# A new order of 1489 tasks for one fused kernel: a long convolution and a state-space scan on one core

## The chip, the cores and the metric

The kernel runs on 1 core of one Trainium2 chip. Its time is device time in microseconds (us), the median of the timed runs. The engines are TensorE (PE, with its weight loads as PEld), VectorE (DVE), ScalarE (ACT), GpSimd (POOL) and SyncE (SP). SP and POOL issue nearly all transfers (DMAs); each engine works through its own instructions in the order in which the program gives them, and waits at one whose inputs or buffers aren't ready.

## The reference

Two independent heads over 2048 positions and 1024 channels, in bfloat16, written side by side into one output:

```
# head A: short convolution, gate, long convolution by FFT, gate
k_shift = sum over t of k_pad[:, t:t+S] * shift_k[:, 3-t]          # 4 taps
kv = k_shift * v
y  = irfft(rfft(kv padded to 2S) * rfft(ssm_k padded to 2S))[:S] + kv * ssm_D
a  = q * y
# head B: diagonal complex state-space layer
Lam_bar = exp(dt * Lam);  B_bar = ((Lam_bar - 1) / Lam) * B
h[t] = Lam_bar * h[t-1] + B_bar x[t]
b  = 2 * Re(C h) + x * Dskip
out = concat(a, b)
```

## The kernel before

The whole kernel is one table, `ORDER`, and a loop over it. Each word of the table is a task (`U.3.0.1`), with the buffers that it takes behind a colon: `p` numbers are the 8 banks of PSUM, `a` numbers the first of one or more 2 KB-per-partition units of an arena of 53 units in SBUF, `h` and `w` numbers three slots each for scanned states (`gslot`) and for constants of the FFT (`wslot`). The loop calls the function of the task, which emits its instructions on the engines; the order of the words is so the order on every engine, and the tile framework puts a wait where an instruction needs another's result or a buffer that is still read.

```
for word in ORDER.split():
    task, _, slots = word.partition(":")
    for code, n in re.findall(r"([a-z])(\d+)", slots):
        cur.setdefault(code, []).append(int(n))
    f, *args = task.split(".")
    E[f](*args)
```

Head B, by blocks of 128 positions (i from 0 to 15):

- `bl`, `bT`, `bc` (or `bcv`): load a block of B (SP), transpose it on PE (8 matmuls against the identity, L415), copy it from PSUM to the tile BT on ACT (L431) or DVE (L427, L429). `cl`, `cT`, `cc`, `cx` do the same for C and the tile CT. `x.i`: a transposing DMA of block i of x (L447).
- `wb`, `wbe`, `exp1`, `dve2`, `sin0`, `eo` and the like make the tables at the start. `eo` is 16 small ACT copies.
- `U.i.jp.jl`: 16 matmuls of 128x128 of x against BT (L464); two of them fill one bank, which `ue` copies to the arena (L473).
- `r1`, `r2`, `cy`, `sc`, `r3`, `r4`: rotation, the scan (L504, one pass per real and imaginary part) and rotation back, on DVE; `cy` carries the state over, on ACT.
- `y` (whole array, L520) or `yq` (four 64x64 quarters of the array at once, L538): the product with CT; `ye` copies it out; `yst`, `ysp`, `ysg`, `ysh` store it (POOL or SP).

Head A, as an FFT of three passes with a bounce through DRAM between each:

- `kp`, `vp` load k and v; `kvm`, `kva`, `kvb`, `kvc` form kv on DVE (L588 to L603); `am` is the first pass on PE (L608), `ae` copies (L614), `ast` stores to Ys_kv (L617). For the filter: `hl`, `hT`, `hc`, `hm` (L657), `he`, `hst` to Ys_h (L668).
- `lh`, `lk` load groups of 128 rows of Ys_h and Ys_kv (L677), `lw` the constants (L672). Each group needs rows of every store. `sh` and `sk` are the second pass (L688), `she` and `ske` copy (L697, L704), `sw` and `swp` swap rows by DMA (L708), `pr` multiplies (L714), `sa` transforms back (L726), `sae` copies, `vst` stores to Vs (L737).
- `vl` loads from Vs (L742), `a3` is the last pass (L754), `a3e` copies (L761), `qp` loads q, `qm` multiplies (L763), `ost` and `osp` store (L764, L765).

A copy out of PSUM stands on ACT; with a `v` behind its name (`saev`, `a3ev`) it stands on DVE. The functions themselves stay as they are; only the table changes.

Of the kernel before, what the change touches and what calls it, by code (L numbers as in the profile page):

```python
# [72 lines left out]
bT.2.1:p0 U.0.0.1 bT.3.0:p7 bc.5.0 bc.2.1 bc.5.1 kva.3 kring U.1.2.0:p5 bl.3.1:a23 cl.0.0:a14 bT.2.0:p2 bT.3.1:p0
bl.7.1:a46 ue.1.0:a34 U.0.2.1:p6 bc.3.1 bc.2.0 U.0.2.0 U.1.2.1 cl.3.0:a37 bl.7.0:a26 cl.1.0:a25 bT.7.1:p2 kvb.3:a22
bT.7.0:p0 ue.0.0:a23 bc.6.1 kp.-2 x.3:a21 U.0.1.0:p3 bc.3.0 gz stt cl.2.0:a12 cT.0.0:p4 bc.7.0 bc.7.1 U.0.1.1 U.0.3.0:p0
kvm.1:a15 ue.1.2 vp.1:a27 U.0.3.1 U.3.2.0:p1 ue.0.1 U.3.0.0:p3 z1 kvm.2:a42 z2 ld_Q U.1.1.1:p2 ue.0.2 ue.0.3 x.2:a52
U.1.1.0 cl.3.1:a13 kva.1 cT.1.0:p7 cl.2.1:a32 kva.2 kvb.1:a14 kvb.2:a39 ue.1.1 kvm.0:a15 rta kvc.3 U.3.0.1 cx.6.0 kva.0
# [5 lines left out]
am.1.0:p7p6 ae.1.1.0 ae.1.0.0 cT.3.0:p5 cx.4.0 r2.3:h2 cx.5.1 r4.0 cx.7.1 hT.0.1:p4 ue.2.0:a36 cx.4.1 cc.3.0 hT.0.4:p2
cy.1:h0 kvm.4:a14 hT.0.6:p7 hc.0.1:a22 am.2.0:p1p3 r1.1:a27 ae.2.1.0 U.2.3.1 ue.2.3 U.2.2.0:p5 kva.4 hc.0.4:a42 U.2.2.1
cx.6.1 ue.2.2 U.2.1.0:p3 cT.2.0:p2 hc.0.6:a32 cc.2.0 ae.2.0.0 U.2.1.1 ast.3 r2.1 ue.2.1 hT.0.2:p5 hT.0.3:p7 ast.1
hc.0.3:a18 hm.0.6.1:p4p2 hT.0.7:p0 he.0.6.1.1:a43 y.0.0.0:p3 y.0.0.1 hm.0.4.0:p2p6 hdv.0 hc.0.7:a12 he.0.6.1.0
hm.0.7.0:p4p1 hT.0.5:p0 he.0.4.0.1:a29 ast.2 hdv.1 sc.1.0 hT.0.0:p7 he.0.4.0.0 hst.0.4.0 hc.0.2:a20 y.0.0.2
he.0.7.0.0:a50 y.0.0.3 hc.0.0:a13 hm.0.6.0:p4p2 ye.0.0:a19 hm.0.4.1:p5p7 y.0.1.0:p6 y.0.1.1 y.0.1.2 y.0.1.3 vp.2:a34
kvb.4:a31 he.0.6.0.0 sc.1.1 he.0.4.1.1 vp.3:a26 r1.2:a14 he.0.4.1.0 he.0.7.0.1 hst.0.7.0 r3.1:a46 hm.0.0.1:p1p5
hst.0.4.1 hc.0.5:a42 he.0.6.0.1 r4.1 hm.0.0.0:p2p3 he.0.0.1.0:a48 cy.2:h1 r2.2 hm.0.5.1:p7p0 ye.0.1 he.0.5.1.1:a23  # L90
he.0.5.1.0 kp.3 he.0.0.1.1 kvm.6:a38 he.0.0.0.0 y.1.1.0:p4 kvc.4 y.1.1.1 hst.0.6.0 hst.0.6.1 kp.4 kva.6 hst.0.5.1
hm.0.5.0:p6p0 he.0.5.0.0 kvm.5:a14 y.1.1.2 he.0.0.0.1 kvb.6:a25 he.0.5.0.1 y.1.1.3 hm.0.7.1:p2p7 ye.1.1:a28 he.0.7.1.0
kva.5 am.4.0:p1p6 y.1.0.0:p4 he.0.7.1.1 x.4:a32 hm.0.3.0:p2p3 ae.4.0.0:a29 hm.0.3.1:p5p0 hst.0.0.1 hst.0.0.0
he.0.3.1.0:a36 kvc.6 y.1.0.1 he.0.3.1.1 hst.0.5.0 kvb.5:a12 sc.2.1 ae.4.1.0 he.0.3.0.1 kvm.7:a13 y.1.0.2 am.4.1:p1p7
hl.3.0:a40 he.0.3.0.0 hm.0.1.0:p5p0 y.1.0.3 he.0.1.0.0:a38 am.6.1:p5p6 ae.4.1.1 U.4.3.1:p7 he.0.1.0.1 ae.6.0.1:a17
hl.2.1:a44 U.4.3.0 kvc.5 ae.6.1.1 am.6.0:p6p5 U.4.0.0:p2 ae.4.0.1 ue.4.3:a23 U.4.1.1:p3 ae.6.0.0 hm.0.2.0:p0p6 ae.6.1.0
ye.1.0 kva.7 hm.0.1.1:p5p7 sc.2.0 hm.0.2.1:p1p4 hst.0.7.1 hl.3.1 he.0.2.0.0:a34 U.4.1.0 he.0.1.1.0 hl.2.0 he.0.2.1.1
# [5 lines left out]
y.2.0.2 kvm.8:a48 r4.3 y.2.0.3 he.1.7.1.0 ae.7.0.1 hc.1.2:a31 y.2.1.3 ye.2.0:a47 hm.1.4.1:p4p6 ae.7.1.1 kva.8
hm.1.7.0:p3p5 ye.2.1 yq.3.0:p1p0 hst.0.1.1 he.1.7.0.1 he.1.7.0.0 hm.1.4.0:p7p2 yst.2 he.1.4.1.0:a29 kvm.9:a39 lw.3:w1
kvb.8:a38 he.1.4.0.1 vp.4:a12 yq.3.1 yq.3.2 he.1.4.1.1 he.1.4.0.0 hm.1.3.0:p5p6 he.1.3.0.1:a15 hm.1.3.1:p3p4 he.1.3.1.0
hst.1.7.0 he.1.3.1.1 yq.3.3 hm.1.2.1:p7p6 x.6:a37 he.1.2.1.0:a19 kva.9 he.1.2.1.1 he.1.3.0.0 kvc.8 x.5:a36 lw.1:w2
kvb.9:a35 kvm.10:a47 U.6.1.0:p3 U.6.1.1 am.8.1:p6p7 ast.7 hst.1.7.1 r1.4:a40 kva.10 ae.8.1.1:a44 hst.1.4.1 ae.8.0.1
# [735 lines left out]
```

## Time and profile before

| | |
|---|---|
| timed runs | 343.4, 344.65, 345.7 us; median 344.65 |
| profiled execution, from first to last instruction | 343.2 us (its own time beside the span isn't given) |
| PE busy | 329.5 us, 5086 matmuls |
| DVE busy | 325.1 us, 263 instructions |
| ACT busy | 273.5 us, 519 instructions |
| POOL busy | 68.9 us, 111 instructions |
| DMA | 100.83 MB, 294 GB/s on average |

All times are of one profiled execution. Busy time is the sum over an engine's instructions; matmuls overlap, so that a start-to-start time tells more of PE than a duration. Lines of the profile give the start and the length of a group of like instructions, the engine, the source line, the operation, output<-input, and in brackets the idle time before it with what ended it.

### The profile page before, as it was taken

What the parts mean: (1) busy time and instruction counts of PE and PEld (TensorE: products, weight loads), DVE (VectorE), ACT (ScalarE), POOL (GpSimd) and SP (SyncE); (2) the same over time, 40 slices, a digit from 0 to 9 for tenths busy, and PEclk for the clock granted to TensorE, in tenths of its full rate; (3) what the DMA queues carried; (4) which work ended last, traced back from release to release, by engine and by line L of the source; (5) the groups of instructions that cost most, each with busy time, mean ns of one, the idle gap of its engine ahead of it and who ended that gap; (6) DMA issues with size and microseconds to landing.
All of it is one profiled execution on the core that took longest, in us unless ns stands there. A gap on an engine that the chain in (4) does not pass through costs nothing.

```text
span 343.2 us, 11813 instructions
## 1 busy us (share of the span) xinstructions
PE 329.5 (96%) x5086; PEld 230.2 (67%) x5105; DVE 325.1 (95%) x263; ACT 273.5 (80%) x519; POOL 68.9 (20%) x111
## 2 busy tenths in 40 slices
...
GB/s 177 352 351 208 315 281 283 155 318 365 368 269 198 264 263 295 233 261 343 313 353 282 270 339 212 369 272 311 280 314 276 216 326 378 327 335 284 375 346 274
DMA packets 62592, 100.83 MB, mean 294 GB/s; under 512 B 29422, under 2 KB 31614, under 8 KB 62540
## 3 DMA queue, kind: packets, MB, share of 16 engines
...
## 4 chain that ended last, share of the span: by engine, by line
PE 74%; ACT 15%; DMA 4%; issue 3%; DVE 3%; SPq 0%; POOL 0%; DVEq 0%; POOLq 0%
PE bank L464 25%; PE bank L538 19%; PE bank L520 10%; PE bank L754 4%; PE bank L688 4%; PE bank L726 4%; PE bank L608 2%; PE bank L657 2%; ACT BT L431 2%; ACT arena L614 2%; ACT arena L473 2%; ACT CT L439 2%; ACT arena L637 2%; DMA wslot<-a_c_W 1%; DMA arena<-arena 1%
## 5 line engine op out<-in xcount | busy, mean ns | idle before, releaser
L464 PEld LDWEIGHTS <-BT 128*128 128x128 bf16 x2048 | 117.8, 98 | 14.4 <-issue 9.9
L464 PE MATMUL bank<-arena,BT 128*128 128x128 bf16 x2048 | 125.4, 221 | 1.1 <-ACT BT L431 0.9
L538 PE MATMUL bank<-CT,gslot 64*64 64x512 bf16 x1408 | 86.6, 378 | 0.0
L504 DVE TENSOR_TENSOR_SCAN gslot<-rtab,gslot 128x1040 bf16<-128x1040 f32 x32 | 73.0, 2311 | 0.5
L538 PEld LDWEIGHTS <-gslot 64*64 64x64 bf16 x1408 | 36.9, 107 | 30.8 <-issue 1.9
L473 ACT CAST arena<-bank 128x512 bf16<-128x512 f32 x63 | 40.5, 660 | 13.8 <-PE bank L464 13.4
L614 ACT CAST arena<-bank 128x512 bf16<-128x512 f32 x64 | 37.2, 680 | 6.7 <-PE bank L608 4.0
L697 ACT CAST arena<-bank 128x512 bf16<-128x512 f32 x63 | 35.0, 617 | 5.9 <-issue 2.8
L520 PE MATMUL bank<-CT,gslot 128*128 128x512 bf16 x153 | 38.5, 380 | 0.3
L665 ACT CAST arena<-bank 128x512 bf16<-128x512 f32 x64 | 35.2, 631 | 3.1 <-PE bank L657 3.0
L714 DVE TENSOR_TENSOR arena<-arena 128x4096 bf16<-128x4096 bf16 x16 | 36.5, 2280 | 1.1 <-DMA arena<-arena 1.0
L487 DVE TENSOR_TENSOR arena<-gslot,Z 128x4096 bf16<-128x4096 bf16 x16 | 36.6, 2287 | 0.8 <-DVE gslot L504 0.2
L704 ACT CAST arena<-bank 128x512 bf16<-128x512 f32 x60 | 34.4, 621 | 3.2 <-PE bank L688 3.0
L734 ACT CAST arena<-bank 128x512 bf16<-128x512 f32 x60 | 32.4, 616 | 5.5 <-PE bank L726 5.3
L487 DVE TENSOR_TENSOR arena<-arena,Z 128x4096 bf16<-128x4096 bf16 x16 | 36.5, 2280 | 0.1
L556 ACT CAST arena<-bank 128x512 bf16<-128x512 f32 x31 | 18.1, 599 | 16.6 <-PE bank L538 8.7
L588 DVE TENSOR_TENSOR arena<-arena 128x4096 bf16<-128x4096 bf16 (+3 forms) x16 | 30.0, 1881 | 0.0
L668 POOL DMA_DIRECT2D Ys_h<-arena x32 | 23.2, 735 | 25.5 <-ACT arena L665 20.2
L617 POOL DMA_DIRECT2D Ys_kv<-arena x16 | 11.2, 726 | 83.5 <-ACT arena L614 81.1
L520 PEld LDWEIGHTS <-gslot 128*128 128x128 bf16 x160 | 14.1, 98 | 15.9 <-issue 2.3
L688 PE MATMUL bank<-arena,wslot 64*64 64x512 bf16 x256 | 21.5, 382 | 0.3 <-DMA wslot<-a_c_W 0.3
L737 POOL DMA_DIRECT2D Vs<-arena x16 | 11.7, 731 | 46.3 <-ACT arena L734 41.3
...
## 6 DMA issues: line engine op xcount, KB each, us to landing
...
```

What stands on the lines that cost most here:

```text
L464: nc.tensor.matmul(pu[:, w, jl, :], BT[:, 2 * jp + jl, w, d, :], xT[:, d, :], start=(d == 0), stop=(d == ND - 1))
L473: cp(st["u", i][:, :, 2 * jp:2 * jp + 2, :], st.pop(("pu", i, jp)))
L487: nc.vector.tensor_mul(m, s_, win(Z))
L504: nc.vector.tensor_tensor_scan(gf, rtab[:].rearrange("p j t -> p (j t)"), gf, 0.0, ALU.mult, ALU.add)
L520: nc.tensor.matmul(py, h[:, w, j, 2:GW], CT[:, j, w, dh * 512:(dh + 1) * 512], start=(j == 0 and w == 0), stop=False)
L538: mm = nc.tensor.matmul(st["py", i, dh][cols, cs(r)], lhs(dh, rows, c), rhs(dh, rows), start=first, stop=last)
L614: cp(st["ysb", n2][:, p, dh * 512:(dh + 1) * 512], st.pop(("pa", n2, p, dh)))
L665: cp(o, st.pop(("pb", hf, s, e, r)).rearrange("p (n c t) -> p n c t", n=2, c=2))
L688: nc.tensor.matmul(st["ps", nm, g, l][64 * dh:64 * dh + 64, :], st["w", i][rows, a * WC:a * WC + 64], st[nm, i][rows, a, dh * 512:(dh + 1) ...
L697: cp(st["hab", i][:, 0, a, l, :], st.pop(("ps", "h", g, l)))
L704: cp(st["x16", i][:, a, l, :], st.pop(("ps", "k", g, l)))
L714: nc.vector.tensor_mul(hab, st.pop(("x16", i)).rearrange("p a l d -> p (a l d)").unsqueeze(1).to_broadcast([P, 2, 2 * D]), hab)
```

## The change

A new table `ORDER`, in which the same tasks stand in another order with other buffers. Of 1489 tasks, 46 have other names than before: copies that go from DVE to ACT or back (20 copies carry the `v` before and 14 after, `bcv` apart), and stores that go by the other of the two queues. Of 670 tasks that name buffers, 58 keep them. The first and the last two lines of the table:

```
-ld_w:a22 wb.3:p3 ld_par wbe.3:a8 par_T:p4 wb.0:p5 wb.7:p1 p32 ld_F bl.1.0:a39 bl.0.1:a18 wb.5:p7 bl.6.0:a34 bl.4.1:a14
+ld_w:a17 wb.7:p1 ld_par par_T:p2 p32 wbe.7:a8 exp1 dd ld_F dve2 wb.5:p0 wbe.5 dve3 tabA1:a15a26a44a37 wb.0:p7 wbe.0
...
-y.15.1.3 ysg.14.1 ost.3 ye.15.1:a1 ysg.15.1 y.15.0.0:p4 y.15.0.1 a3e.15.0 y.15.0.2 qm.7 osp.7 y.15.0.3 ye.15.0 ysh.15.0
+y.15.1.3 y.14.0.3 qp.2:a17 a3e.7.0 qm.3 ye.15.1 ye.14.0 ost.7 ost.0 qm.1 qm.2 osp.2 osp.1 ysh.15.1 ysh.14.0 ysg.15.0
+ost.3
```

Since the table is one line longer, every line number of the kernel after it is one higher than before.

On SP, at the start, behind the five small loads of parameters: the loads of B (`bl`, L420), of x (`x`, L447, transposing) and of k (`kp`, L570). Before:

```order
L420 DMA arena<-in_B_B_im_dram 128x1024
L420 DMA arena<-in_B_B_re_dram 128x1024
L447 DMA_TRANSPOSE arena<-in_B_x_dram 128x8x128
L570 DMA arena<-in_A_k_dram 128x2048
L420 DMA arena<-in_B_B_im_dram 128x1024
L570 DMA arena<-in_A_k_dram 128x2048
L447 DMA_TRANSPOSE arena<-in_B_x_dram 128x8x128
```

And now:

```order
L421 DMA arena<-in_B_B_im_dram 128x1024 x2
L421 DMA arena<-in_B_B_re_dram 128x1024 x3
L421 DMA arena<-in_B_B_im_dram 128x1024
L421 DMA arena<-in_B_B_re_dram 128x1024
L571 DMA arena<-in_A_k_dram 128x2048
L421 DMA arena<-in_B_B_im_dram 128x1024
L571 DMA arena<-in_A_k_dram 128x2048
L421 DMA arena<-in_B_B_re_dram 128x1024
L421 DMA arena<-in_B_B_im_dram 128x1024
L448 DMA_TRANSPOSE arena<-in_B_x_dram 128x8x128
```

Before, three more loads of B stand ahead of the piece that is shown, so that the first load of x is the sixth large one; now it is the thirteenth.

On DVE, at the start, behind the small operations on parameters: `bcv.1.1` (L427, to the tile BT), `kvm.3` (L588) and what follows. Before:

```order
L342 SCALAR_TENSOR_TENSOR b_224<-pm_222,rden 128x16
L427 TENSOR_SCALAR BT<-bank_102 128x1024
L588 TENSOR_TENSOR arena<-arena 128x4096
L429 COPY BT<-bank_96 128x1024
L595 TENSOR_TENSOR arena<-arena 128x2048
```

And now:

```order
L343 SCALAR_TENSOR_TENSOR b_235<-pm_233,rden 128x16
L589 TENSOR_TENSOR arena<-arena 128x4096
L428 TENSOR_SCALAR BT<-bank_102 128x1024
L596 TENSOR_TENSOR arena<-arena 128x2048
L430 COPY BT<-bank_100 128x1024
```

Both copies to BT stand one place later.

On DVE, the end, behind the last scan: `r3.15` (L487), `r4.15` (L510), copies out of PSUM (L761, L556) and the products with q (L763). Before:

```order
L487 TENSOR_TENSOR arena<-gslot_89,Z_78 128x4096
L510 TENSOR_TENSOR gslot_89<-arena 128x16x128
L761 CAST arena<-bank_98 128x512
L763 TENSOR_TENSOR arena<-arena 128x2048 x3
L761 CAST arena<-bank_99 128x512
L761 CAST arena<-bank_103 128x512
L763 TENSOR_TENSOR arena<-arena 128x2048 x2
L761 CAST arena<-bank_99 128x512
L763 TENSOR_TENSOR arena<-arena 128x2048 x2
```

And now:

```order
L488 TENSOR_TENSOR arena<-gslot_91,Z_78 128x4096
L762 CAST arena<-bank_101 128x512
L762 CAST arena<-bank_102 128x512
L511 TENSOR_TENSOR gslot_91<-arena 128x16x128
L762 CAST arena<-bank_96 128x512
L764 TENSOR_TENSOR arena<-arena 128x2048 x3
L557 CAST arena<-bank_101 128x512
L764 TENSOR_TENSOR arena<-arena 128x2048 x3
```

Behind `r4.15` stand two copies and six products now, four copies and seven products before.

Around the second bounce the table reads as follows before (`am.12.1` is the last task of the first pass over kv, `lk.1` the first load behind the bounce, `sk.3` its first use):

```
am.12.1:p6p0 lh.3:a1 ae.14.1.1 ae.12.0.0:a41 ae.12.1.1 U.8.3.1 U.8.2.1:p4 r1.6:a32 ae.12.0.1 ae.15.1.1 ae.12.1.0
ue.8.3:a38 sc.5.0 sh.2:p0p2 U.8.1.1:p1 U.8.1.0 she.2.0:a48 U.9.0.1:p5 ue.8.1 sh.3:p3p7 ast.14 sc.5.1 she.2.1 she.3.0
she.3.1 ast.15 sh.7:p0p1 she.7.0:a11 U.9.0.0 swp.1.0 she.7.1 U.8.2.0 r2.6:h2 U.9.1.0:p0 sh.1:p6p1 ue.9.0:a30 sh.6:p7p5
sh.0:p2p3 U.9.1.1 she.6.1 ue.8.2 r3.5:a19 U.10.3.1:p5 U.10.3.0 ast.12 she.6.0 she.1.0:a40 r4.5 she.0.0 ue.9.1 r1.7:a44
lk.1:a9 U.9.2.0:p7 U.9.3.0:p4 she.0.1 ue.10.3:a19 sk.3:p2p5 sk.2:p6p0
```

And now:

```
am.12.1:p2p0 sc.5.0 ae.12.0.0 U.8.1.0 ae.12.1.1
ae.12.0.1 U.8.3.1 ue.8.3:a48 ysp.4 ue.8.1 U.9.0.1:p1 sh.7:p4p2 r1.6:a14 lw.0:w0 sh.0:p3p6 she.7.0:a10 she.0.1:a38
she.7.1 she.0.0 lh.1:a0 lw.1:w2 ast.14 sh.2:p5p0 U.8.2.1:p7 r3.5:a43 ast.12 she.2.0:a4 U.8.2.0 ue.8.2 she.2.1 r2.6:h1
U.9.2.1:p6 sh.3:p4p2 she.3.1 sh.1:p5p3 sh.6:p0p7 she.6.0 she.6.1 sw.3.0 sw.3.1 she.3.0 sw.1.1 U.9.0.0 ue.9.0:a22 she.1.0
she.1.1 sw.0.0 U.10.3.0:p2 lh.8:a33 U.9.2.0 ue.9.2 U.9.3.0:p4 U.9.3.1 r4.5 cy.6 sw.0.1 r1.7:a14 lk.1:a28 sk.2:p5p7
```

More of the change, by code (lines that the diff above doesn't have):

```diff
@@ L73 @@
[L73 to L77, printed above, removed]
@@ L83 @@
[L83 to L87, printed above, removed]
@@ L88 @@
[L88 to L97, printed above, removed]
@@ L103 @@
[L103 to L107, printed above, removed]
@@ new lines @@
+bl.0.0:a40 bc.0.1 wb.4:p5 wbe.4 bl.1.0:a50 bT.1.0:p4 tabA2 bc.1.0 sin0 bl.2.0:a33 bT.2.0:p0 bl.5.1:a21 bl.6.0:a13
+bT.0.0:p3 kp.1:a0 bl.1.1:a14 sin1 bT.5.1:p1 kp.0 bc.0.0 par_rest bl.5.0:a12 bT.1.1:p6 bl.2.1:a46 bT.6.0:p4 kvm.3:a39
+bcv.1.1 bT.5.0:p3 bT.2.1:p7 x.0:a19 U.0.0.1:p2 sin2 eo bc.2.0 bc.5.1 bc.2.1 kp.-1 x.1:a34 bl.6.1:a32 kva.3 bcv.6.0
+U.0.0.0 ue.0.0:a28 bl.3.0:a17 bc.5.0 kvb.3:a13 bT.6.1:p4 U.1.0.1:p6 U.1.0.0 bc.6.1 bl.4.0:a25 bT.4.0:p2 bT.3.0:p7 stt
+bc.4.0 cl.1.1:a14 bc.3.0 kring kvm.1:a39 bl.3.1:a12 U.0.1.0:p0 bl.7.0:a33 bT.7.0:p3 bT.3.1:p5 bc.7.0 U.0.3.0:p1
@@ new lines @@
+ue.1.0:a32 vp.1:a30 bc.3.1 kvm.2:a43 bl.7.1:a18 U.0.2.0:p7 bT.7.1:p2 bc.7.1 kvc.3 U.0.2.1 am.3.1:p5p6 ue.0.2 kp.-2
+kvm.0:a20 am.3.0:p4p3 z1 ae.3.0.1:a37 ae.3.1.0 ae.3.0.0 ae.3.1.1 kva.2 U.0.3.1 ue.0.3 rta cl.1.0:a50 kva.1 x.3:a52
+U.3.2.1:p7 U.3.1.1:p2 kvb.2:a48 kvb.1:a18 kvc.2 kva.0 ld_Q U.0.1.1 ue.0.1 U.3.0.0:p5 r1.0:a40 kvb.0:a25 U.1.2.1:p3 z2
+U.3.0.1 ue.3.0:a26 am.2.1:p0p1 ae.2.0.1:a15 cT.1.0:p4 cc.1.0 gz r2.0:h1 vp.0:a35 kvc.1 U.3.2.0 ue.3.2 ae.2.1.1 kvc.0
+U.1.2.0 ue.1.2 cT.1.1:p0 cx.6.1 ast.3 cc.1.1 U.3.1.0 ue.3.1 cl.0.0:a31 kp.2 cT.0.0:p7 cc.0.0 cl.2.0:a51 cx.5.0
@@ new lines @@
+ue.2.3 U.2.0.1 hc.0.2:a31 cx.4.0 hm.0.6.1:p4p0 he.0.6.1.1:a28 hdv.0 hT.0.0:p7 he.0.6.1.0 hc.0.0:a46 hT.0.4:p3 ue.2.0
+hT.0.3:p1 hc.0.3:a18 hT.0.1:p4 r2.1 hc.0.1:a39 ast.2 hT.0.5:p6 hc.0.5:a33 hT.0.7:p0 hc.0.7:a48 kvm.4:a35 y.0.0.0:p5
+y.0.0.1 cx.5.1 y.0.0.2 hst.0.6.1 kp.3 U.2.1.0:p4 sc.1.0 cx.4.1 hc.0.4:a15 hm.0.6.0:p1p7 hm.0.0.0:p0p6 he.0.0.0.0:a16
+he.0.0.0.1 sc.1.1 kva.4 he.0.6.0.0 he.0.6.0.1 hst.0.6.0 y.0.0.3 hst.0.0.0 r3.1:a42 U.2.1.1 hm.0.7.0:p2p0 kvb.4:a24
+ue.2.1 hm.0.4.1:p1p3 he.0.4.1.1:a50 he.0.4.1.0 hst.0.4.1 hm.0.4.0:p7p6 ye.0.0:a49 r4.1 cx.6.0 cx.7.0 y.0.1.0:p4
```

188 lines of the change are left out of this document (97 added, 91 removed).

## The prediction

> **What bounds the kernel now.** I read the busy times and the chain on the page first, then the busy times by stretch, then the instructions of TensorE (PE) in order of time.
>
> ```profile
> PE 329.5 (96%) x5086; PEld 230.2 (67%) x5105; DVE 325.1 (95%) x263; ACT 273.5 (80%) x519; POOL 68.9 (20%) x111
> PE 74%; ACT 15%; DMA 4%; issue 3%; DVE 3%; SPq 0%; POOL 0%; DVEq 0%; POOLq 0%
> 0.00:20.00 20.00, 14.28 (x107) 11.17 (x108) 13.62 (x36) 16.92 (x35) 5.62 (x17) 1.00 0.89 281
> 20.00:40.00 20.00, 19.95 (x355) 19.76 (x354) 19.89 (x29) 19.20 (x26) 0.00 (x0) 1.00 1.17 262
> 320.00:343.20 23.20, 17.95 (x90) 8.38 (x90) 15.88 (x15) 9.44 (x18) 4.37 (x7) 0.94 0.89 323
> ```
>
> PE is 96% busy and makes 74% of the chain that ended last; VectorE (DVE) is as full, but is 3% of that chain. In the stretch rows (columns: length, then PE, PEld, DVE, ACT, POOL) PE lacks 5.7 us in the first 20 us and 5.2 in the last 23.2; the 300 us in between hold the other 297.3 of its 329.5. An order of tasks can only win in three places: the start, PE's short waits in between, and the end.
>
> A busy PE need not be PE at full speed, so I look at the time from start to start (columns: start, length; idle before it in brackets).
>
> ```profile
> 3.72 0.58 PE L402 MATMUL bank<-arena,ones 1*128 1x512 bf16 x1 [3.72 <-DMA arena<-in_A_shift_k_dram]
> 7.47 4.45 PE L415 MATMUL bank<-ident,arena 128*128 128x128 bf16 x40
> 13.07 1.01 PE L415 MATMUL bank<-ident,arena 128*128 128x128 bf16 x8 [1.15 <-ACT BT L431]
> 14.93 1.89 PE L464 MATMUL bank<-arena,BT 128*128 128x128 bf16 x16 [0.85 <-ACT BT L431]
> 20.80 1.50 PE L415 MATMUL bank<-ident,arena 128*128 128x128 bf16 x24
> 22.14 1.06 PE L464 MATMUL bank<-arena,BT 128*128 128x128 bf16 x16
> 23.03 0.61 PE L415 MATMUL bank<-ident,arena 128*128 128x128 bf16 x8
> ```
>
> At 7.47 us, 40 transposes take 4.45 us, 111 ns each; at 20.80 us, 24 of them start within 1.34 us, 56 ns each. A U task (16 matmuls of L464) takes 1.89 us at 14.93 and 0.89 us at 22.14 (next start 23.03). So PE runs at half speed until about 20 us, though the column of the granted clock (the third from the end) says 1.00 there. From 20 us on, U tasks run at 56 ns a matmul and gaps are rare: PE's work itself is the bound.
>
> **The change, part by part.** The work is the same. *The six copies.* Counted in the task table, 20 copies out of PSUM stand on DVE before and 14 after (the two `bcv` apart, in both).
>
> ```profile
> L761 ACT CAST arena<-bank 128x512 bf16<-128x512 f32 x23 | 12.4, 592 | 6.4 <-PE bank L754 4.5 <-PE bank L523 1.9
> L761 DVE CAST arena<-bank 128x512 bf16<-128x512 f32 x9 | 5.9, 679 | 0.0
> ```
>
> By these two rows DVE loses 6 x 0.68 = 4.1 us, and ACT gains 6 x 0.59 = 3.6 us. I cost both at nothing: PE's stream hides them, and ACT is idle for a fifth of the span. Were that cover gone, ACT's 3.6 us would be the price.
>
> *Switches on PE.* Some tasks use PE as four 64x64 quarters (`yq`, `hm`, `sh`, `sk`, `sa`), the others whole.
>
> ```profile
> 225.42 1.07 PE L464 MATMUL bank<-arena,BT 128*128 128x128 bf16 x16
> 226.42 0.41 PE L688 MATMUL bank<-arena,wslot 64*64 64x512 bf16 x4
> 226.66 0.82 PE L538 MATMUL bank<-CT,gslot 64*64 64x512 bf16 x12
> 231.32 0.43 PE L688 MATMUL bank<-arena,wslot 64*64 64x512 bf16 x4
> 231.68 1.06 PE L464 MATMUL bank<-arena,BT 128*128 128x128 bf16 x16
> ```
>
> A U task that a quarter task follows takes 1.00 us (225.42 to 226.42), not 0.89: 0.11 us for the change of shape. Back again, L688 takes 0.36 us (231.32 to 231.68) where it takes 0.24 before another quarter task (226.42 to 226.66): 0.12. The table has 76 such changes before and 70 after: 6 x 0.11 = **-0.65 us**. Nothing hides it, since PE is the bound.
>
> *The start.* x.0 (the first transposed block of x) stands sixth among SyncE's large loads before, thirteenth after; DVE's `bcv.1.1` goes behind `kvm.3`; and ten weight transposes (`bT`), not six, run ahead of the first U.
>
> ```profile
> 4.87 1.33 SPq L447 DMA_TRANSPOSE arena<-in_B_x_dram  x1
> DMA to landing us min/median/max: 3.6/6.7/7.3
> 14.21 0.68 DVE L427 TENSOR_SCALAR BT<-bank 128x1024 bf16<-128x1024 bf16 x1
> 14.81 2.28 DVE L588 TENSOR_TENSOR arena<-arena 128x4096 bf16<-128x4096 bf16 x1
> 19.41 1.92 ACT L431 ACTIVATE BT<-bank 128x1024 bf16<-128x1024 bf16 x2
> 21.89 2.85 ACT L431 ACTIVATE BT<-bank 128x1024 bf16<-128x1024 bf16 x3 [0.57 <-PE bank L415]
> ```
>
> Four more `bT` at 8 x 111 ns are 3.56 us; they fill the two idle pieces of 1.15 and 0.85 us; so the first U starts at 14.93 + 3.56 - 2.00 = 16.5 us. x.0 is issued seven places of some 0.47 us later (the first landing row is that of L447): 8.2 us, landed by 14.9 at the median and 15.5 at most, so it hides behind the transposes with 1 us to spare, and costs what it is later than that. `bcv.1.1`, by the two DVE rows, ends at about 14.2 + 2.2 + 0.7 = 17.1; only the second half of that U needs it, which begins at 17.4. Full speed came 4.9 us after the first U before (14.93 to about 19.8), so about 21.4 after. Half speed lasts 1.6 us longer (costs 0.8), but 2.0 us that were idle are worked at half speed (gains 1.0). Against that, `bT.4.0` now stands in the PSUM bank of the first U, which ACT empties only behind three BT copies that follow the 16 small copies of `eo`. Those 16 ended at 19.41 before; one BT copy (0.95, a third of 2.85) stands ahead of them in addition now, so 20.4; three more make 23.2, the bank's own copy (0.59) 23.8. PE is out of work at 23.1: full speed from 21.4 leaves it two U. So 0.7, and 0.2 for a second bank wait behind it, 0.9 together. Sum: **+0.7 us**. Bounds: -1.5, if no bank wait comes and the clock rises no later; +3, if x.0 lands 2 us late as well.
>
> The Trainium skill ("TensorE: Matmul & The Clock Gate", Part 1) says that about 3.4 us of sustained activity lift the clock from half to full; its Part 4 says that transposes don't count. The trace sides with Part 4: PE is unbroken from 3.72 to 11.9 us and stays at 111 ns. By Part 1 alone the new unbroken start would be at full speed before its first U; that is a rival below.
>
> *The short waits.* These are PE's own rows in the list of waits, the 0.3 us ones, all after 20 us; and one of them in place.
>
> ```profile
> PE bank L688 <- DMA wslot<-a_c_W: 0.3, 1, 0.3
> PE bank L608 <- DVE arena L603: 0.3, 1, 0.3
> PE bank L726 <- DVE arena L714: 0.3, 1, 0.3
> PE bank L608 <- ACT CT L439: 0.3, 1, 0.3
> PE bank L657 <- ACT arena L665: 0.3, 1, 0.3
> 246.56 0.39 PE L538 MATMUL bank<-CT,gslot 64*64 64x512 bf16 x4
> 247.29 0.62 PE L688 MATMUL bank<-arena,wslot 64*64 64x512 bf16 x8 [0.34 <-DMA wslot<-a_c_W]
> ```
>
> The five sum to 1.5 us. The one at 247.29 costs more than its 0.34: 0.73 us from start to start, where 0.24 would do, so 0.5. With 0.15 more for each they are worth 2.25. They go if the new order covers each, and new ones may come: bounds -2.25 and +2.25. I take somewhat over half, **-1.3 us**, since two of the five wait for DVE, which has 4.1 us less to do.
>
> *The bounces through DRAM.* Three times all stores must land before the first load.
>
> ```profile
> 156.05 1.41 POOL L617 DMA_DIRECT2D Ys_kv<-arena  x2 [1.41 <-ACT arena L614]
> 162.46 0.98 SPq L677 DMA_DIRECT2D arena<-Ys_kv  x2
> 167.69 0.63 PE L688 MATMUL bank<-arena,wslot 64*64 64x512 bf16 x8
> DMA to landing us min/median/max: 4.4/5.5/11.6
> L614 ACT CAST arena<-bank 128x512 bf16<-128x512 f32 x64 | 37.2, 680 | 6.7 <-PE bank L608 4.0 <-issue 1.6 <-remote 0.6
> ```
>
> Here the last store of the second bounce is issued at about 156.8, the first load at 162.46, and PE uses it at 167.69, 5.2 us later, about what such loads take (the landing row is that of L677). Between `am.12.1`, the last producer, and the first `sk` stand 13 U and 6 `sh` before, 11 U and 6 `sh` after: 2 x 0.89 = 1.8 us less cover. ACT's copies of group 12 have two copies of other groups among them before and none after, which gives 2 x 0.68 = 1.4 back: **+0.4 us**, bounds 0 and +6.1 (a load of 11.6 us in place of 5.5). The third bounce gains cover: from `sa.27` to the first `a3` PE has 16.7 us of work before and 20.2 after. No wait shows there now, so I count nothing.
>
> *The end.*
>
> ```profile
> 337.83 0.22 PE L523 MATMUL bank<-Dd,arena 128*128 128x128 bf16 x1
> 338.09 0.58 ACT L556 CAST arena<-bank 128x512 bf16<-128x512 f32 x1 [2.60 <-PE bank L523]
> 338.70 0.34 SPq L560 DMA_DIRECT2D out_dram<-arena  x1
> ```
>
> PE's last matmul, one ACT copy, one store of half a block, and the landing: 343.2 - 338.05 = 5.15 us. The new table ends with the same four steps. Behind `r4.15` DVE has two copies and six products left, not four and seven, and PE three blocks of y: **0**, bounds -1 and +1.
>
> **Sum.** 343.2 + 0.7 - 0.65 - 1.3 + 0.4 = 342.35 us of span. The profiled execution's own time isn't given beside its span; the three timed runs (343.4, 344.65, 345.7) lie 0.2 to 2.5 us above it, their median 1.45. So 342.35 + 1.45 = **343.8 us**.
>
> **The rivals.** *Waits all go* (0.21): no new wait appears, no bank wait at the start, and the wider bounces also cut the spread of the runs: 343.2 - 2.25 - 0.65 - 1.5 (the start's lower bound) = 338.8, plus 1.2, 340.0 us. For it: PE has no other bound. Against it: the DMA share (the column before the last) is 0.89 to 1.17 in the stretches shown, so landings will still scatter. *The early clock* (0.04): the U tasks of 16.5 to 21.4 us run at full speed, 2.4 us less, 341.4. Against it: the 111 ns over 8 us. *The second bounce comes late* (0.15), the slower one: `lk.1` takes 11.6 us, as one such load did before, with 1.8 us less cover: 343.8 + 5.7 = 349.5. It decides from the point where the load lands after PE has run through the 11 U and 6 `sh` behind `am.12.1`; before, the use came 5.2 us after the issue, with nothing to spare. *The change moves only what PE's stream hides*: 343.2 - 0.65 + 1.45 = 344.0, not to be told from the forecast; the two hold 0.60.
>
> **Chances and range.** A measurement of this kernel can tell some 1% from no change, here 3.4 us: below 341.2 or above 348.1. Faster 0.21, same 0.64 (forecast, hidden moves, early clock), slower 0.15. The range reaches into both outer rivals: 340.0 at the low end; above, the forecast with the start's upper bound, 343.8 + 2.3 = 346.1, and part of a late load, 347.4.
>
> **What would show it.** The first L464 of U at 16 to 17 us, and transposes at 56 ns from 21 to 22 us; 14 copies on DVE; a wait of PE for ACT near 23 us; PE's waits after that under 2 us in all; no wait of L688 for Ys_kv near 167 us; the last matmul 5 us before the end. The prediction is wrong if PE idles over 3 us after 25 us, or if the first U starts below 14 us.

## The result, and the profile after

| | before | after |
|---|---|---|
| median of 20 runs | 344.44 us (342.70 to 346.88) | 347.15 us (345.03 to 349.74) |
| ratio, 95% interval | | 1.0069 (1.0047 to 1.0091) |
| profiled execution, span | 343.2 us | 343.4 us (its own time 345.14) |

The new table is slower, by 2.4 us by the ratio. That is less than the 1% that the prediction took for measurable, but with 20 runs a side the interval leaves out 1. The forecast was 343.8: inside its range (340.0 to 347.4) the time came out near the upper end, and on the other side of the old table. The two profiled executions hide this: their spans differ by 0.2 us. The one of after is among the two shortest of 20 (the middle span is 345.4), so three more were profiled, below.

The page of after (busy times, then the chain that ended last) and its busy times by stretch, in the columns of the prediction:

```profile
PE 329.1 (96%) x5105; PEld 230.9 (67%) x5105; DVE 321.7 (94%) x257; ACT 276.9 (81%) x525; POOL 70.3 (20%) x113
PE 76%; DMA 11%; ACT 8%; SPq 1%; issue 1%; DVE 1%; POOL 1%; ACTq 0%; POOLq 0%; DVEq 0%
0.00:20.00 20.00, 13.71 (x121) 9.55 (x121) 14.83 (x39) 17.04 (x34) 5.65 (x17) 1.00 0.88 266
20.00:40.00 20.00, 18.36 (x306) 17.46 (x307) 20.00 (x28) 19.97 (x29) 0.70 (x1) 1.00 1.16 285
320.00:343.40 23.40, 18.92 (x99) 8.84 (x96) 13.28 (x13) 7.72 (x14) 5.43 (x8) 1.00 0.78 285
```

Each engine's work is close to what the prediction counted: DVE 3.4 us less (4.1 counted), ACT 3.4 us more (3.6 counted), PE the same. What changed is what PE waits for: DMA has 11% of the chain, 4% before. PE's instructions at the start, in order of time:

```profile
6.93 1.89 PE L416 MATMUL bank<-ident,arena 128*128 128x128 bf16 x16
9.28 4.72 PE L416 MATMUL bank<-ident,arena 128*128 128x128 bf16 x48
14.92 1.32 PE L416 MATMUL bank<-ident,arena 128*128 128x128 bf16 x16 [0.91 <-DMA arena<-in_B_B_re_dram]
16.57 0.62 PE L465 MATMUL bank<-arena,BT 128*128 128x128 bf16 x8 [0.33 <-DMA arena<-in_B_x_dram]
17.35 1.51 PE L465 MATMUL bank<-arena,BT 128*128 128x128 bf16 x24 [0.16 <-DVE BT L428]
21.42 0.62 PE L416 MATMUL bank<-ident,arena 128*128 128x128 bf16 x8 [2.56 <-DMA arena<-in_B_B_im_dram]
```

The first U starts at 16.57, as forecast (16.5), but at once at full speed: its first 8 matmuls take 0.62 us, where 16 took 1.89 before. Then PE stands 2.56 us for one load of B, `bl.6.1`. SP's rows show why it is late:

```profile
9.38 2.69 SPq L448 DMA_TRANSPOSE arena<-in_B_x_dram  x1
13.21 2.25 SPq L448 DMA_TRANSPOSE arena<-in_B_x_dram  x1
15.50 0.59 SPq L421 DMA_DIRECT2D arena<-in_B_B_im_dram  x1
```

The two transposing loads of x hold SP for 2.69 and 2.25 us here (1.33 and 1.74 before), and the load of B comes behind both. What this wait costs is another question; the run `t_start` answers it below.

### The profile page after: what moved, and what is told of

Same layout as the page of the kernel before. It is cut to its first block, busy times and chain, and to the rows that moved or that the text cites. A ratio compares the mean times of both kernels' runs of the same rounds, so it can differ in the third digit from the quotient of the medians.

```text
span 343.4 us, 11813 instructions
## 1 busy us (share of the span) xinstructions
PE 329.1 (96%) x5105; PEld 230.9 (67%) x5105; DVE 321.7 (94%) x257; ACT 276.9 (81%) x525; POOL 70.3 (20%) x113
## 4 chain that ended last, share of the span: by engine, by line
PE 76%; DMA 11%; ACT 8%; SPq 1%; issue 1%; DVE 1%; POOL 1%; ACTq 0%; POOLq 0%; DVEq 0%
PE bank L465 28%; PE bank L539 17%; PE bank L521 9%; PE bank L755 4%; PE bank L689 3%; PE bank L727 3%; PE bank L609 3%; DMA arena<-in_A_ssm_k_dram 3%; DMA wslot<-a_c_W 3%; PE bank L633 2%; PE bank L416 2%; PE bank L658 2%; DMA arena<-in_B_B_im_dram 2%; ACT arena L698 2%; ACT arena L735 1%; DMA arena<-in_A_k_dram 1%
## 5 line engine op out<-in xcount | busy, mean ns | idle before, releaser
L465 PEld LDWEIGHTS <-BT 128*128 128x128 bf16 x2048 | 116.6, 98 | 12.7 <-issue 7.8
L465 PE MATMUL bank<-arena,BT 128*128 128x128 bf16 x2048 | 123.9, 219 | 0.5 <-DMA arena<-in_B_x_dram 0.3
L539 PEld LDWEIGHTS <-gslot 64*64 64x64 bf16 x1408 | 37.8, 107 | 28.5 <-ACT arena L705 1.5
L474 ACT CAST arena<-bank 128x512 bf16<-128x512 f32 x64 | 39.4, 626 | 10.6 <-PE bank L465 10.2
L615 ACT CAST arena<-bank 128x512 bf16<-128x512 f32 x64 | 34.6, 635 | 6.7 <-PE bank L609 6.7
L705 ACT CAST arena<-bank 128x512 bf16<-128x512 f32 x61 | 34.1, 622 | 5.2 <-PE bank L689 4.9
L488 DVE TENSOR_TENSOR arena<-arena,Z 128x4096 bf16<-128x4096 bf16 x16 | 36.5, 2284 | 1.5 <-ACT arena L474 1.4
L488 DVE TENSOR_TENSOR arena<-gslot,Z 128x4096 bf16<-128x4096 bf16 x16 | 36.6, 2287 | 0.2
L698 ACT CAST arena<-bank 128x512 bf16<-128x512 f32 x63 | 34.3, 629 | 2.3 <-PE bank L689 2.0
L557 ACT CAST arena<-bank 128x512 bf16<-128x512 f32 x30 | 17.7, 609 | 21.4 <-PE bank L539 11.7
L735 ACT CAST arena<-bank 128x512 bf16<-128x512 f32 x63 | 33.4, 610 | 1.6 <-PE bank L727 1.3
L666 ACT CAST arena<-bank 128x512 bf16<-128x512 f32 x64 | 33.2, 618 | 1.2 <-PE bank L658 1.1
L689 PE MATMUL bank<-arena,wslot 64*64 64x512 bf16 x256 | 21.4, 383 | 0.6 <-DMA wslot<-a_c_W 0.6
```

The costliest lines, as they stand in the source:

```text
L465: nc.tensor.matmul(pu[:, w, jl, :], BT[:, 2 * jp + jl, w, d, :], xT[:, d, :], start=(d == 0), stop=(d == ND - 1))
L474: cp(st["u", i][:, :, 2 * jp:2 * jp + 2, :], st.pop(("pu", i, jp)))
L488: nc.vector.tensor_mul(m, s_, win(Z))
L539: mm = nc.tensor.matmul(st["py", i, dh][cols, cs(r)], lhs(dh, rows, c), rhs(dh, rows), start=first, stop=last)
L615: cp(st["ysb", n2][:, p, dh * 512:(dh + 1) * 512], st.pop(("pa", n2, p, dh)))
L666: cp(o, st.pop(("pb", hf, s, e, r)).rearrange("p (n c t) -> p n c t", n=2, c=2))
```

## The experiments

**Three more executions of the new table, one of the old.**

> The new table unchanged, profiled once more. Its profiled execution so far had a span of 343.4 us, among the two shortest of 20 (343.3 to 348.0, their middle 345.4). Theory (late loads): the typical execution carries about 2 us more of waits of PE than that profile, and they stand where PE already waited for a transfer there: for the late load of B at 18.9 us (2.56), for the filter load near 88 us, for wslot constants near 191 and 248 us, for the swap near 243 us. Rival 1 (second bounce): the extra time is one wait of L689 for Ys_kv near 167 us, 2 us or more. Rival 2 (clock): the first stretch takes longer because the transposes and the first U tasks run at 111 ns for longer, with no more waits.

> The same table once more, for the scatter of its waits. Theory (late loads): PE's waits for DMA sum to 9 to 13 us (8.6 in the first profile), at the same four places, with different lengths in each execution. Rival 1 (second bounce): a wait for Ys_kv near 167 us. Rival 2 (clock): the first matmul at 56 ns comes later than 16.5 us.

> The same table a third time. Theory (late loads): whichever of the three looks has the longest span has the largest sum of PE's waits for DMA at the four places. Rival 1: at the second bounce. Rival 2: a later full clock at the start.

> The old table unchanged, profiled again. Its profiled span (343.2 us) was near the middle of its 20 runs, so this one should agree within 1 us. Theory (late loads): no single wait of PE over 1 us after 25 us, and PE's waits for DMA after 25 us below 1.5 us. Rivals: the old table's own start or bounces vary by as much as the new one's.

Their spans are 346.4, 349.0 and 344.8 us for the new table and 341.3 for the old (expected within 1 us of its first profile, it is 1.9 shorter). PE's waits from the list of waits (total, times, longest), for the first profile of the new table, then its longest execution:

```profile
PE bank L633 <- DMA arena<-in_A_ssm_k_dram: 0.6, 1, 0.6
PE bank L689 <- DMA wslot<-a_c_W: 0.6, 2, 0.4
PE bank L727 <- DVE arena L715: 0.6, 1, 0.6
```

```profile
PE bank L689 <- DMA wslot<-a_c_W: 2.7, 3, 1.1
PE bank L633 <- DMA arena<-in_A_ssm_k_dram: 1.5, 1, 1.5
PE bank L465 <- ACT arena L615: 0.9, 1, 0.9
PE bank L539 <- issue: 0.6, 1, 0.6
PE bank L727 <- DVE arena L715: 0.5, 1, 0.5
```

and all that the second profile of the old table lists there:

```profile
PE bank L608 <- DVE arena L603: 0.3, 1, 0.3
PE bank L657 <- ACT arena L665: 0.2, 1, 0.2
```

With one more row of 0.2 us in each of the other five, PE waits 2.0, 4.6, 6.4 and 2.2 us after 25 us in the four profiles of the new table (the two not shown have L633 1.5, L689 1.4, L465 1.0, L727 0.5, and L689 1.5, L727 0.5), and 1.7 and 0.5 us in the two of the old. That is 3.8 against 1.1 on average, and the longer the execution, the more it waits. Take each execution's waits off its span, and 341.4, 341.8, 342.6 and 342.6 us are left for the new table, 341.5 and 340.8 for the old: the spans are 3.65 us apart on average, these rests 0.95. In two of the four PE waits over 3 us after 25 us, which the prediction had named as a sign of being wrong. The first rival falls: in none of the four does PE wait for Ys_kv near 167 us. The second falls as well: in all four the first U runs at full speed.

The wait near 92 us (L633, the filter's transposes) can be followed back. Engine by engine, in `after_look2`:

```profile
46.96 2.29 DVE L488 TENSOR_TENSOR arena<-arena,Z 128x4096 bf16<-128x4096 bf16 x1 [1.37 <-ACT arena L474]
77.38 0.69 DVE L602 TENSOR_TENSOR arena<-arena 128x1024 bf16<-128x1024 bf16 x1
78.09 4.01 SPq L624 DMA_DIRECT2D arena<-in_A_ssm_k_dram  x4
arena<-in_A_ssm_k_dram SPq DMA_DIRECT2D x4, 512.0 KB, 11.6
92.53 1.13 PE L633 MATMUL bank<-ident,arena 128*128 128x128 bf16 x15 [1.54 <-DMA arena<-in_A_ssm_k_dram]
```

DVE waits at 46.96 for a copy of ACT, then has no idle time up to L602, which reads the buffer last; only then can SP issue the filter loads, which land 11.6 us later. So DVE, not PE, sets when these loads can start. How long PE then waits is the landing's doing too: L602 starts at 77.32 to 77.38 in three of the four executions, and PE goes on at 91.53, 92.45 and 92.53; in `after_look3` L602 starts at 78.08, and PE doesn't wait at all (91.48).

**Covering PE's waits, place by place.** `t_start` moves one load, `t_mid` covers two places of the middle, `t_late` those after 185 us, `t_all` is all three.

```diff
 t_start
-x.0:a19 U.0.0.1:p2 sin2 eo bc.2.0 bc.5.1 bc.2.1 kp.-1 x.1:a34 bl.6.1:a32 kva.3
+bl.6.1:a32 x.0:a19 U.0.0.1:p2 sin2 eo bc.2.0 bc.5.1 bc.2.1 kp.-1 x.1:a34 kva.3
 t_mid
-hT.1.7:p0 hc.1.7:a22 hT.1.2:p3 hc.1.2:a28 U.4.2.1:p4 cy.3 sc.3.1 sc.3.0 U.4.2.0
+U.4.2.1:p4 U.4.2.0 hT.1.7:p0 hc.1.7:a22 hT.1.2:p3 hc.1.2:a28 cy.3 sc.3.1 sc.3.0
-ue.5.3:a28 U.7.1.1 kvb.11:a15 ae.9.1.1 ae.9.0.1 ae.9.1.0
+U.7.1.1 kvb.11:a15 ae.9.1.1 ae.9.0.1 ae.9.1.0 ue.5.3:a28
 t_late
-swp.2.0 swp.2.1 yq.6.7 ye.6.1:a4 sh.10:p4p3 she.10.1 lw.4:w0
+lw.4:w0 swp.2.0 swp.2.1 yq.6.7 ye.6.1:a4 sh.10:p4p3 she.10.1
-lk.11:a41 ... sw.9.0 ... sw.9.1 ... x.12:a33 ... sh.21:p3p5 ... U.12.0.0:p1 ... U.12.0.1
+lk.11:a41 x.12:a33 ... swp.9.0 ... swp.9.1 ... U.12.0.0:p1 U.12.0.1 sh.21:p3p5
```

> The new table with one word moved: the load bl.6.1 goes on SP ahead of the transposing load x.0 instead of behind x.1. In the four profiles of the new table PE waits 2.5 to 2.6 us for it before the L416 at 21.1 to 21.4 us. Theory (late loads): that wait goes, PE meets the second x block with at most 0.7 us of wait, and the new table gains 1.8 to 2.6 us (so it stands 0 to 1 us above the old one, not 2.7). Rival (DVE and ACT take the gain back): PE reaches its later waits for DVE and ACT earlier and the end moves by less than 0.8 us.

> The new table with two PE waits of the middle covered: the two U.4.2 tasks go ahead of hT.1.7 and hT.1.2 (which wait 0.6 to 1.5 us for the filter loads near 92 us), and the ACT copy ue.5.3, which waits 1.5 us for a store of Ys_h in two of four profiles, goes behind the copies ae.9. Theory (late loads): PE's wait of L633 is 0 to 0.3 us, no L465 waits for ACT near 130 us, gain 0.8 to 2.2 us. Rival (give-back): a gain below 0.5 us, with a longer wait of PE for DVE or ACT later.

> The new table with the late waits covered: the constants lw.4 go on SP ahead of the two swaps of group 2; the swaps sw.9.0 and sw.9.1 go on SP instead of behind two stores on POOL; x.12 is loaded some 30 tasks earlier; U.12.0.0 and U.12.0.1 go ahead of sh.21, so that lw.10 has 1.8 us more. Theory (late loads): the waits of L689 for wslot near 192 and 248 us (0.2 and 0.4 us in the first profile, 0.5 to 1.1 in the others) and of L727 for DVE near 243 us (0.5 to 0.6) go; gain 1.5 to 2.5 us. Rival (give-back): below 0.7 us, because DVE's chain of scans then holds PE up further on.

> All edits of the three kernels t_start, t_mid and t_late together. Theory (late loads): the gains add, 4 to 7 us against the new table, so 340 to 343 us, 1.5 to 4 us below the old one; PE's waits after 18 us sum to 1 to 4 us, as with the old table. Rival (give-back): the sum is under 2.5 us, the time stays within 1 us of the old one.

| | median | ratio to before (95%) |
|---|---|---|
| t_start | 346.43 | 1.0071 (1.0044 to 1.0097) |
| t_mid | 346.82 | 1.0081 (1.0058 to 1.0104) |
| t_late | 350.05 | 1.0178 (1.0151 to 1.0206) |
| t_all | 351.19 | 1.0201 (1.0171 to 1.0230) |

By the ratio, the first two gain nothing on the new table's 1.0069: there the give-back rival holds. The other two lose, which neither expectation had. In t_mid's own profile both covered waits are gone; PE waits 3.0 us after 25 us, and the span is 345.1. In t_start the 2.5 us wait went as well. PE, ACT and DVE, in time order:

```profile
21.18 1.95 PE L465 MATMUL bank<-arena,BT 128*128 128x128 bf16 x32 [0.30 <-DMA arena<-in_B_x_dram]
23.12 0.59 ACT L474 CAST arena<-bank 128x512 bf16<-128x512 f32 x1
23.76 1.05 PE L416 MATMUL bank<-ident,arena 128*128 128x128 bf16 x16 [0.63 <-ACT arena L474]
77.36 0.68 DVE L602 TENSOR_TENSOR arena<-arena 128x1024 bf16<-128x1024 bf16 x1
90.73 0.23 PE L633 MATMUL bank<-ident,arena 128*128 128x128 bf16 x1
92.94 1.13 PE L633 MATMUL bank<-ident,arena 128*128 128x128 bf16 x15 [1.98 <-DMA arena<-in_A_ssm_k_dram]
```

and the same three places in the first profile of the new table, with the wait for `bl.6.1`:

```profile
23.09 0.57 ACT L474 CAST arena<-bank 128x512 bf16<-128x512 f32 x1
23.71 1.05 PE L416 MATMUL bank<-ident,arena 128*128 128x128 bf16 x16
90.70 0.22 PE L633 MATMUL bank<-ident,arena 128*128 128x128 bf16 x1
```

Nothing was saved: PE's next transposes (`bT.4.0`, L416) need the bank of the first U, and ACT's copy (L474) frees it at 23.7 us either way. With `bl.6.1` in time, PE waits there for ACT instead, 0.63 us; the rest of the 2.5 us went into waits for x and, in this execution, into a first U at half speed (32 matmuls in 3.20 us). PE reaches the filter's transposes at 90.7 us in both, so the longer wait at 92.94 is a later landing and not a gain given back, as the expectations of the next runs have it. Only in `after_look3`, where half clock followed the wait, does PE pass the bank later, at 24.95.

t_late lost part of its time by a new neighbour on SP. Its swaps on SP, what SP waited for between them (a line's instructions: nanoseconds, then the first and the last start), and DVE:

```profile
236.73 0.47 SPq L709 DMA_DIRECT2D arena<-arena  x1
L709 SPq EVENT_SEMAPHORE  x1: 4703/4703/4703, 237.2 to 237.2; - x1
242.31 1.11 SPq L709 DMA_DIRECT2D arena<-arena  x2
245.73 2.29 DVE L715 TENSOR_TENSOR arena<-arena 128x4096 bf16<-128x4096 bf16 x1 [4.90 <-DMA arena<-arena]
```

`swp.9.0` goes at 236.73; then stands `swp.11.0`, which waits 4.7 us for its own rows; `swp.9.1`, moved from POOL to SP, is behind it and goes last. DVE waits 4.90 us for the swaps, where it waited 2.02 to 2.95 in the four profiles of the new table, and PE stands 1.62 us for DVE behind it. That is not all of the loss: PE also waits 1.03 us for ACT at 214.49 and 1.10 us for the copy of a U bank at 257.59, two places where it waits in none of the four. When I wrote the next expectations I blamed the transposing load x.12 ahead of them; these rows refute that.

**DVE's idle time, and the late edits in another form.**

```diff
 t_dve
-r1.3:a22 r3.0:a36
+r3.0:a36 r1.3:a22
-r1.5:a3 ast.15 ue.7.0 kvb.12:a10
+kvb.12:a10 r1.5:a3 ast.15 ue.7.0
 t_dve_start: t_dve and t_start
 t_swap
-vst.8 ... vst.4 ... sw.9.0 ... sw.9.1
+sw.9.0 sw.9.1 vst.8 vst.4
-lw.11:w1 ... x.12:a33 ... sh.21:p3p5 ... U.12.0.0:p1 ... U.12.0.1 ue.12.0:a42
+x.12:a33 lw.11:w1 ... U.12.0.0:p1 U.12.0.1 ue.12.0:a42 sh.21:p3p5   (and lw.4 as in t_late)
 t_best: t_start, t_mid, t_dve and t_swap
```

> The new table with two pairs of DVE tasks swapped: r3.0 ahead of r1.3, and kvb.12 ahead of r1.5. In the new table DVE idles 1.1 to 1.4 us before r1.3 (near 46 us) and 1.0 to 1.4 us before r1.5 (near 151 us), each time for an ACT copy of U, and has no idle time from there to 92 us, where PE waits for filter loads whose buffer DVE releases. Theory (DVE and ACT hold PE: what PE saves early it loses again at the filter loads): L633 near 92 us comes 0.8 to 1.4 us earlier and the time falls by 0.7 to 2 us. Rival (PE's own stream is the bound and DVE's idle time is cover): no change, under 0.5 us.

> The two swaps of t_dve and the load bl.6.1 ahead of x.0 (t_start) together. t_start alone moved the time by -0.7 us, since PE, 2 us earlier at 21 us, waited 2.1 us for the filter loads at 92.9 us. Theory (DVE holds PE): with DVE 1.1 to 1.4 us earlier too, the two gains add to more than the parts, 2 to 3 us. Rival (PE alone): what t_start gave, 0.7 us. Third (the load's landing, not its issue, sets L633): L633 stays at 92 to 93 us, under 1 us.

> The late edits once more, in another form. t_late was 2.9 us slower than the new table: there x.12, a transposing load, had come to stand just ahead of the three swaps on SP, whose issue then took 6.7 us, and DVE waited 4.9 us for them. Here the swaps sw.9.0 and sw.9.1 stay on POOL, but ahead of the two stores vst.8 and vst.4; x.12 stands behind lh.15, six microseconds ahead of the next swap; lw.4 ahead of the swaps of group 2, U.12.0 with its copy ahead of sh.21 as in t_late. Theory (swaps behind a transposing load are what t_late lost): the swaps land 1 to 1.5 us earlier than in the new table, DVE waits under 1 us for them, gain 1 to 2.5 us against the new table, 4 to 5 against t_late. Rival (U.12.0 ahead of sh.21 is what t_late lost): it stays 2 us or more slower than the new table.

> All edits of t_start, t_mid, t_dve and t_swap in one table. Theory (PE, DVE and ACT hold one another, and each gain counts once the others keep up): 4 to 7 us below the new table, 340 to 343 us, that is 1 to 4 us below the old one. Rival (waits only move): within 1.5 us of the new table.

| | median | ratio to before (95%) |
|---|---|---|
| t_dve | 346.09 | 1.0041 (1.0014 to 1.0068) |
| t_dve_start | 346.04 | 1.0031 (1.0005 to 1.0057) |
| t_swap | 349.67 | 1.0120 (1.0069 to 1.0172) |
| t_best | 349.86 | 1.0135 (1.0094 to 1.0177) |

t_dve_start is the best of the new table's kin, some 1.3 us below it by the ratios; its profile shows a shorter chain to 92 us:

```profile
45.66 2.29 DVE L488 TENSOR_TENSOR arena<-gslot,Z 128x4096 bf16<-128x4096 bf16 x1
76.20 0.68 DVE L602 TENSOR_TENSOR arena<-arena 128x1024 bf16<-128x1024 bf16 x1
76.91 3.74 SPq L624 DMA_DIRECT2D arena<-in_A_ssm_k_dram  x4
90.74 1.18 PE L633 MATMUL bank<-ident,arena 128*128 128x128 bf16 x16
```

DVE no longer waits near 46 us, L602 comes 1.16 us earlier than in t_start, and all 16 transposes of L633 run without a wait. PE reaches them at 90.74, as before, so what came earlier are the loads. In this execution the theory's mechanism is seen: DVE holds the filter loads, and with them PE. Its 2 to 3 us was too much, and that the parts add up is not shown: t_dve and t_dve_start can't be told apart by their intervals, and the bank at 23.7 us takes what t_start's word saves (PE waits 0.78 us for ACT at 23.73 here). Nor does t_dve's own profile, its slowest run of twelve, show the mechanism: DVE waits 1.44 us for a load of v at 72.61, and L602 comes at 78.83.

t_best, and t_swap with it, lost by a buffer: `vst.4` stores from the unit that the ACT copy `ske.22.1` writes next, and I had put it behind the swaps. ACT, PE and the granted clock (the third column from the end) in t_best:

```profile
242.43 2.05 ACT L705 CAST arena<-bank 128x512 bf16<-128x512 f32 x4 [2.24 <-DMA Vs<-arena]
243.56 0.85 PE L727 MATMUL bank<-arena,wslot 64*64 64x512 bf16 x7 [1.94 <-ACT arena L705]
243.80:247.20 3.40, 3.40 (x41) 2.01 (x37) 3.19 (x3) 1.92 (x6) 0.00 (x0) 0.50 0.92 251
247.20:250.00 2.80, 2.80 (x64) 2.32 (x60) 0.78 (x1) 2.80 (x6) 0.72 (x1) 0.99 0.48 151
```

PE stood 1.94 us, and the next 3.4 us ran at half clock: a wait of 2 us cost up to 3.6. What the same store cost in t_swap's time isn't known: t_late_b, which leaves it where it was, can't be told from t_swap by its interval (below).

**Is it ACT that holds the others?** ACT is busy for 47.88 of the 48 us from 12 to 60 us in the new table, for 47.20 in the old. `a_pool` and `b_pool` put five table operations on POOL, in the new table and in the old; `a_pool_ds` adds the edits of t_dve_start; `t_late_b` is t_swap without its edit on POOL.

```diff
-z1: nc.scalar.mul(...)      z2: nc.scalar.copy(...) x2, nc.scalar.mul(...)             rta: nc.scalar.copy(...)
+z1: nc.gpsimd.tensor_scalar z2: nc.gpsimd.tensor_copy x2, nc.gpsimd.tensor_scalar      rta: nc.gpsimd.tensor_copy
```

> The new table with five operations on tables in SBUF (z1, the three of z2, the copy of rta) on POOL instead of ACT. In the new table ACT is busy without a gap from 12 to 60 us, DVE waits 1.1 to 1.4 us for its copies near 46 us, and POOL idles from 7 to 34 us; the five take ACT 4.75 us from start to start between 30.8 and 38.5 us. Theory (ACT holds DVE and PE over the first 60 us): DVE's wait before r1.3 goes, the filter loads land earlier, 1 to 2.5 us less. Rival (PE's own stream is the bound): no change, under 0.5 us. Third (POOL is so slow, or so disturbs DVE, that the tables come late): slower.

> The same five operations on POOL, in the old table, where ACT is as full (7.2 to 8.0 of each 8 us from 12 to 60 us). Theory (ACT holds the others in the first 60 us): 0.5 to 2 us below the old table. Rival (PE's stream alone is the bound): within 0.5 us.

> The new table with the five operations on POOL (a_pool) and the edits of t_dve_start, which alone gave about 1.3 us. Theory (ACT, DVE and PE hold one another): 2.5 to 4 us below the new table, so level with the old one or up to 1.5 us below it. Rival (the gains are the same gain): no more than the better of the two parts.

> The late edits without those of the swaps on POOL: lw.4 ahead of the swaps of group 2, x.12 behind lh.15, U.12.0 with its copy ahead of sh.21; sw.9 and the stores stay where the new table has them. In t_swap vst.4 had come behind sw.9, and the ACT copy ske.22.1, which reuses the buffer that vst.4 stores from, held ACT for some 2 us and PE with it. Theory (that store was what t_swap lost): 0.5 to 2 us below the new table, the waits of L689 near 192 and 248 us gone. Rival (U.12.0 ahead of sh.21 is the loss): 2 us or more above the new table, with a wait of PE behind U.12.0.

a_pool 356.55 (1.0372), b_pool 354.49 (1.0311), a_pool_ds 355.71 (1.0336): the third case, and it says nothing on ACT. POOL and DVE in a_pool:

```profile
23.70 14.96 POOL L358 TENSOR_SCALAR Z<-Z 128x1024 bf16<-128x1024 bf16 x1 [18.25 <-DVE Z L356]
38.63 0.10 POOL L377 MEMSET rtab<- 128x16 f32 x1
38.68 1.03 POOL L378 COPY rtab<-r 128x1024 f32<-128x1024 f32 x1
38.70 3.16 DVE L488 TENSOR_TENSOR arena<-arena,Z 128x4096 bf16<-128x4096 bf16 x1 [2.67 <-POOL Z L358]
```

One product takes POOL 14.96 us, and DVE waits for it. The copy beside it takes 1.03. t_late_b (347.98, 1.0102, 1.0068 to 1.0137) can't be told from the new table, and neither of its expectations held: its waits at 192 and 248 us went, and PE waited 0.9 us for Ys_h at 277 us instead.

So copies alone, early, behind `kring`: `a_act` on t_dve_start, `b_act` on the old table.

```diff
-z2: nc.scalar.copy(...) x2, nc.scalar.mul(...)   rta, in its place: nc.scalar.copy(...)
+z2: nc.scalar.mul(...)    behind kring: rta z2p   (three nc.gpsimd.tensor_copy)
```

> t_dve_start with three table operations on POOL instead of ACT, early (behind kring): the copy of rta and the two copies of z2. In a_pool the product z1 took 15.0 us on POOL and was waited for 2.7 us by DVE and 5.6 us on behind; rta's copy took 1.0 us and the two of z2 4.0 us there. ACT saves 2.85 us before 40 us. Theory (ACT holds DVE and PE over the first 60 us): 0.7 to 2 us below t_dve_start, so about the old table's time or up to 1 us below. Rival (DVE, slowed while POOL works, gives it back; or PE alone is the bound): level with t_dve_start (1.2 us above the old table) or slower.

> The same three operations on POOL, early, in the old table. Theory (ACT holds the others): 0.5 to 1.5 us below the old table, which would make it the fastest of all. Rival: within 0.5 us, or slower where DVE runs slower beside POOL.

a_act 345.38 (1.0046, 1.0020 to 1.0072), level with t_dve_start; b_act 347.15 (1.0101, 1.0066 to 1.0136). The same stretch in t_dve_start, then in a_act:

```profile
36.00:44.00 8.00, 7.68 (x125) 7.16 (x125) 8.00 (x7) 7.97 (x12) 0.00 (x0) 1.00 1.03 270
```

```profile
36.00:44.00 8.00, 8.00 (x130) 7.29 (x128) 8.00 (x7) 6.25 (x10) 0.00 (x0) 1.00 1.12 209
```

ACT has 1.7 us of idle time now, and nothing comes of it. PE is 0.6 us earlier at its first filter transposes (54.71 against 55.29 us) and then waits 0.76 us at 60.44 for an ACT copy whose buffer a store still reads. So the gain that the theory named did not come; that ACT holds DVE and PE behind `kring` is not borne out. Ahead of it the theory wasn't tested, and there ACT does hold PE: 0.71 us at 23.81 in a_act too, for the bank of the first U. Why b_act is slower than the old table stays open; its profile has the clock at half for more of the start (0.62 on average from 12 to 20 us) and waits of 1.6 us for Ys_kv.

No version beat the old table.

## Why the prediction was wrong, by its own steps

- **The bound.** The three places where an order can win or lose were right. That PE's work alone is the bound was not: DVE, which I read as 3% of the chain, has no idle time from 50 to 77 us, and its L602 says when the loads for PE's place at 92 us can start (t_start against t_dve_start). A 3% share of the chain meant that DVE was just in time, not that it had slack.
- **The six copies, 0.** DVE and ACT moved by 3.4 us each, where the rows said 4.1 and 3.6. That it costs nothing was not tested alone.
- **Switches, -0.65.** The number of changes is as counted; the term was not measured alone.
- **The start, +0.7: right in size, partly by luck.** If every matmul that starts before 29.75 us is priced at its spacing at full speed, PE has done 16.9 us of work before and 16.2 after (17.7 in the second profile of the old table, 14.8 in `after_look3`). The bank wait was right in its time: I had the bank free at 23.8, it is free at 23.7, and PE goes on behind it at 23.71 to 23.77 in three of the four profiles. What I had ahead of it was not: the clock was early, not late, and the time so won went into the wait for `bl.6.1`. Those two errors cancelled. I had counted x.0's place on SP at 0.47 us for each load ahead of it, and had not followed the loads behind the transposing ones. The rival "early clock" had a chance of 0.04; its condition came true, its 341.4 us did not. The Trainium skill ("TensorE: Matmul & The Clock Gate", Part 1) has the clock rise after about 3.4 us of sustained activity. The U at full speed at 16.57, after 64 transposes from 6.93 us with one other matmul among them, goes against my reading of Part 4; but the 3.4 us don't fit either, since PE ran without a break from 3.60 us and 48 transposes from 9.28 still took 4.72 us, so that by the two spacings some 34 of them were at 111 ns.
- **The short waits, -1.3, bounds of 2.25 either way: this step failed.** They came to 2.0, 4.6, 6.4 and 2.2 us after 25 us, 3.8 on average. That is 2.1 more than in the profile that the term was priced from (1.7), just inside the upper bound, and 2.7 more than the average of both old profiles (1.1), outside it; so 3.4 or 4.0 us from what I took. The miss of the whole is 3.35. I priced the five waits that one profile of the old order showed and assumed that a new order would cover somewhat over half. A new order makes its own; where its loads stand on SP, and which buffer each takes, was there to read.
- **The bounces, +0.4.** No wait for Ys_kv near 167 us in any of the four profiles: 0. The end: 343.4 - 338.9 = 4.5 us behind the end of PE's last matmul, where 5.15 were counted: some 0.7 less, within its bounds.
- **From span to median.** I added 1.45 us; the old table's median stands 1.24 above its profiled span, the new one's 3.8. One profile of a kernel whose waits depend on landings can be its best case.
- **The rivals** lacked the one that came: loads that are later than their uses at several places at once.

Part of this stays open. The added waits are seen directly, and without them the spans of the two tables are 0.95 us apart instead of 3.65; but no edit took them all away, so that they are the cause of that part is read from six profiles and not shown by a run.
